# A state-space scan and a bilinear feed-forward on one core: longer down-weight rows, pair 2 turned later, seven small loads more

## The chip, the cores and the metric

The kernel runs on one core of one Trainium2 chip. Its time is the device time of one execution in microseconds (us); a version's time is the median over its runs. Five engines work side by side, each through its own instructions in order: TensorE (PE, with its weight loads shown as PEld), VectorE (DVE), ScalarE (ACT), GpSimd (POOL) and SyncE (SP), which here only issues DMAs. They meet at semaphores.

## The reference, cut to what matters

Inputs are `x` (4 batches, 8 heads, 768 steps, 32 wide), decays `a`, and `B`, `C` (16 states). The first part is a scan in chunks; per batch and head

```python
L = exp(cum[i] - cum[j]) * (i >= j)            # cum = cumsum(log a) in the chunk
y = (C @ B.T * L) @ x + (C @ state) * exp(cum)
state = decay_full * state + (B * decay_from_j).T @ x
```

The result, one row of 256 (8 heads of 32) for each of 3072 tokens, goes into a feed-forward part:

```python
a = y @ w_a          # 256 -> 1536
b = y @ w_b
out = (a * b) @ w_out   # 1536 -> 256
```

The order of the 1536 middle columns is free, as long as `w_a`, `w_b` and `w_out` agree on it.

## The kernel before

**Tiling.** A sequence is cut into 6 blocks of 128 steps, and two batches are taken together: 12 pairs `p` (`NP`), pair `p` being block `p // 2` of batches 2(p % 2) and the next. Per pair, in this order:

- `load(p)` (line 128): six DMAs on SP, two each for `bn`, `cn`, `xn` (64, 64 and 128 KB each). Three buffers of each.
- `scale(p)` (254): POOL multiplies `cn` and `bn` by the decay factors into `cm` and `bm` (in this order) and turns `xn` into f16.
- `transposes(p)` (259): four transposes on PE, of `bm` first, then `cm`. With `ct_first` DVE copies `ct` and then ACT writes `bt` in two operations; the `bt` operations wait for that `ct`.
- `scores(p)` (285): 32 small matmuls, which need `ct` and `bt`, into four banks `SC[0..3]`.
- `mask(product(p, m))` (318): DVE multiplies one bank by the causal mask; with `by_pool` ACT copies the bank out and POOL multiplies.
- `pv(p)` (362): PE forms the scan's output in the banks of `SC[2]` and `SC[3]`, so it starts after the masks of these have read them; then the sums for the state; then ACT writes `X2T` of the pair (line 383). `state(p)` follows on DVE and POOL.
- Six `unit(p, k2)` (462): 4 matmuls of 128x256 with `Wa` into a bank `aps`, 4 with `Wb` into `bps` (line 437), ACT copies `aps` to `asb` (451), DVE multiplies `bps` by `asb` into `hk` (458). `go` runs whole units. They need `X2T`.
- `out_mm` (468): 12 down products for each of the pair's two batches into a bank `ops`, `out_store` (480): ACT scales it into `osb`, SP stores it (488).

The banks `aps`, `bps`, `ops` are four of one pool (`psf`); a bank is used again when its last reader is done.

**Weights.** `Wa`, `Wb` are kept in halves of 768 columns, each loaded and cast by a POOL DMA (`load_w`), `Wo` in two halves of 6 x 256 (`load_wo`). Middle columns are dealt out so that a partition of `Wo` holds three neighbouring rows of `w_out` (3 KB in a row); the up products therefore pick every third column of `W` as their 128 weights:

```python
W[k // 6][:, f, k % 6 // 3 * 384 : (k % 6 // 3 + 1) * 384].rearrange("p (c kk) -> p kk c", kk=3)[:, k % 3]
```

**Order.** It is written out by hand (`manual_schedule`): each engine runs its instructions in the order in which the Python code records them, SP's DMAs too. Lines 590 to 627 hold the start-up of pairs 0 to 3, in which units of pairs 0 and 1 stand between the stages of pair 2; from line 629 a loop over `p` from 3 on repeats one pattern. SP's order in the start-up is: `x` of pair 2 (held until `Wb`'s second half has landed, line 579), `load(3)`, `load(4)`, the two stores of pair 0, `load(5)`, the two stores of pair 1, and so on.

Of the kernel before, what the change touches and what calls it, by code (L numbers as in the profile page):

```python
# [9 lines left out]
f32 = mybir.dt.float32  # L10
# [5 lines left out]
AFTER = mybir.DependencyInfo(mybir.DependencyClass.Sync, mybir.DependencyReason.DATA)  # L16
# [6 lines left out]
def kernel(  # L23
# [13 lines left out]
    nc = tc.nc  # L37
# [7 lines left out]
    NK = d_ff // 128  # L45
# [19 lines left out]
    const = ctx.enter_context(tc.tile_pool(name="const", bufs=1))  # L65
# [16 lines left out]
    Wo = big.tile([128, NK, d_model], f16, name="Wo")  # L82
# [37 lines left out]
    def load1(eng, p, which, bt, i0=0, n=64):  # L120
        blk, bp = divmod(p, NBP)
        src = (B, C, x)[which][2 * bp + bt, :, blk * Q + 2 * i0 : blk * Q + 2 * i0 + 2 * n, :]
        return eng.dma_start(  # L123
            pair_in[p][which][64 * bt + i0 : 64 * bt + i0 + n].rearrange("i h r n -> i h (r n)"),
            src.rearrange("h (i r) n -> i h (r n)", r=2),
        )

    def load(p, eng=None):
        tiles(p)
        return [load1(eng or nc.sync, p, w, bt) for w in range(3) for bt in range(2)]  # L130
# [7 lines left out]

    def load_wo(half):
        nc.gpsimd.dma_start(  # L140
            Wo[:, 6 * half : 6 * half + 6].rearrange("p (g kk) e -> p g (kk e)", kk=3),
            moe_w_out.rearrange("(g p kk) e -> p g (kk e)", p=128, kk=3)[:, 2 * half : 2 * half + 2],
        )

    nc.sync.dma_start(a_sb, a.rearrange("b h (k q) -> (b h) k q", q=Q))
# [36 lines left out]
    load1(nc.gpsimd, 1, 0, 1)  # L182
    load1(nc.gpsimd, 1, 1, 0)
    load_w(0)
    for bt in range(2):
        load1(nc.gpsimd, 1, 2, bt)

    def warmup(n, bank, cols=512):
        for _ in range(n):
# [69 lines left out]
    def transposes(p, ps=None, between=None, ct_first=False):  # L259
        s = st[p]  # L260
        TB, TC = (TT[:, 0:256], TT[:, 256:512]) if ps is None else [t_.bitcast(f16)[:, 0:256] for t_ in ps]
        for T_, src in ((TB, s["bm"]), (TC, s["cm"])):
            for r in range(2):
                nc.tensor.transpose(  # L264
                    T_[:, r * 128 : (r + 1) * 128], src[:, r].rearrange("p h n -> p (h n)"), ident
                )
            if between:
                between()
                between = None
        BT = mid.tile([128, 2, 2, 2, 64], f16, name="bt", tag="bt")  # L270
        CT = mid.tile([128, 2, Q], f16, name="ct", tag="ct")

        def ct(copy):
            copy(CT.rearrange("p t (i r) -> p r (t i)", r=2), TC.rearrange("p (r c) -> p r c", r=2))  # L274

        if ct_first:
            ct(nc.vector.tensor_copy)
        for e in range(2):
            o_ = BT[:, e].rearrange("p r t i -> p (r t i)")
            nc.scalar.activation(out=o_, in_=TB, func=AF.Copy, scale=par[:, e : e + 1])  # L280
        if not ct_first:
            ct(nc.scalar.copy if ps is None else nc.vector.tensor_copy)
        s["BT"], s["CT"] = BT, CT
# [20 lines left out]
    def product(p, m):  # L304

        return (
            st[p]["T1"][:, 2 * m : 2 * m + 2].rearrange("p e r q -> p e (r q)"),
            SC[m].rearrange("p (e c) -> p e c", e=2),
        )
# [8 lines left out]
    def mask(out_in, by_pool=False):  # L318
        o_, i_ = out_in
        c_ = causal.rearrange("p r q -> p (r q)").unsqueeze(1).broadcast_to((128, 2, 2 * Q))  # L320
        if by_pool:
            tmp = mid.tile([128, 2, 2 * Q], f32, name="tmp", tag="tmp")
            nc.scalar.copy(tmp, i_)
            nc.gpsimd.tensor_tensor(out=o_, in0=tmp, in1=c_, op=ALU.mult)
        else:
            nc.vector.tensor_tensor(out=o_, in0=i_, in1=c_, op=ALU.mult)  # L326
# [35 lines left out]
    def pv(p, then=None):  # L362
        blk, bp = divmod(p, NBP)
        s = st[p]
        PY = [SC1[:, bt, 0:256] for bt in range(2)]
        if blk > 0:
            for bt in range(2):
                for u in range(2):
                    nc.tensor.matmul(  # L369
                        PY[bt][:, u * Q : (u + 1) * Q],  # L370
                        s["Sbd"][:, bt, u * 128 : u * 128 + 128],
                        s["CT"][:, bt],
                        start=(u == 0),
                        stop=False,
                        skip_group_check=True,
                    )
        for u in range(2):
            pv_u(p, u, PY, blk == 0)
        if blk < NBLK - 1:
            ds_mm(p, 256)  # L380
        if then:
            then()
        nc.scalar.activation(  # L383
            out=X2T[:, p].rearrange("p u t q -> p t u q"),
            in_=SC1[:, :, 0:256].rearrange("p t (u q) -> p t u q", u=2),
            func=AF.Copy,
            scale=YS / XS,
        )
# [43 lines left out]
    def unit_mm(p, k2, W):  # L432
        ps = psf.tile([128, 512], f32, name="aps" if W is Wa else "bps", tag="ff")
        for kk in range(2):
            k = 2 * k2 + kk
            for f in range(2):
                nc.tensor.matmul(  # L437
                    ps[:, kk * 2 * Q : (kk + 1) * 2 * Q],
                    W[k // 6][:, f, k % 6 // 3 * 384 : (k % 6 // 3 + 1) * 384].rearrange("p (c kk) -> p kk c", kk=3)[
                        :, k % 3  # L440
                    ],
                    X2T[:, p, f].rearrange("p t q -> p (t q)"),
                    start=(f == 0),
                    stop=(f == 1),
                    skip_group_check=True,
                )
        return ps
# [14 lines left out]
    def unit(p, k2):  # L462
        a_ps = unit_mm(p, k2, Wa)
        b_ps = unit_mm(p, k2, Wb)
        asb = evac_a(a_ps)
        return lambda: times(p, k2, b_ps, asb)

    def out_mm(p, bt, o_ps, ks):
        hk = st[p]["hk"]
        for k in ks:  # L470
            nc.tensor.matmul(  # L471
                o_ps[:, 0:d_model],
                hk[:, k, bt * Q : (bt + 1) * Q],
                Wo[:, k, :],
                start=(k == 0),
                stop=(k == NK - 1),
                skip_group_check=True,
            )

    def out_store(p, bt, o_ps, on_dve=False, q=None):  # L480
        blk, bp = divmod(p, NBP)
        o_sb = ffh.tile([128, d_model], f32, name="osb", tag="osb")
        if on_dve:
            nc.vector.tensor_scalar(o_sb, o_ps[:, 0:d_model], 1.0 / (YS * YS), None, ALU.mult)
        else:
            nc.scalar.activation(out=o_sb, in_=o_ps[:, 0:d_model], func=AF.Copy, scale=1.0 / (YS * YS))  # L486
        r0 = (2 * bp + bt) * S + blk * Q
        (q or nc.sync).dma_start(out[r0 : r0 + Q, :], o_sb)
# [13 lines left out]
    def go(*items):  # L502
        for p, k2 in items:
            unit(p, k2)()
# [70 lines left out]
        op=ALU.mult,  # L575
    )
    load_wo(1)
    x2 = [load1(nc.sync, 2, 2, bt) for bt in range(2)]
    tc.add_manual_dep(x2[0].ins, w1[1].ins.name, AFTER, reason="weights ahead of pair 2's x")
    for m in range(3):  # L580
# [18 lines left out]
    state_spread(0)  # L599
    state_spread(1)  # L600
    load(3)
    go((0, 3), (0, 4))
    transposes(2, ct_first=True)
    go((1, 3), (0, 5))
    scores(2)
    mask(product(2, 3), by_pool=True)
    h = unit(1, 4)
    mask(product(2, 0))
    h()
    mask(product(2, 1))  # L610
    h = unit(1, 5)
    mask(product(2, 2))
    h()
    scale_x(2, nc.scalar)
    scale(3)
    o = [bank("ops"), bank("ops")]
    for bt in range(2):
        out_mm(0, bt, o[bt], range(6))
    pull(2)
    pv(2)  # L620
    transposes(3, ct_first=True)
    state(2)
    fb(2)
    load(4)
    for bt in range(2):
        out_mm(0, bt, o[bt], range(6, NK))
        out_store(0, bt, o[bt])

    for p in range(3, NP):
        scores(p)  # L630
        if p + 1 < NP:
            scale(p + 1)
        if p + 2 < NP:
            load(p + 2)
        h = unit(p - 1, 0)
        mask(product(p, 0))
        h()
        mask(product(p, 1))
        mask(product(p, 2))
        h = unit(p - 1, 1)  # L640
        h()
        mask(product(p, 3))
        go((p - 1, 2))
        out_half(p - 2, 0)
        go((p - 1, 3))
        pull(p)
        pv(p)
        state(p)
        if p + 1 < NP:
            transposes(p + 1)  # L650
        out_half(p - 2, 1)
        if p % 2 == 0 and p // 2 + 1 < NBLK:
            fb(p // 2 + 1)
        go((p - 1, 4), (p - 1, 5))
# [6 lines left out]
    o = [psf.tile([128, 512], f32, name="ops", tag="ff") for _ in range(2)]  # L661
# [35 lines left out]
```

## Time and profile before

| | |
|---|---|
| median of 10 runs | 132.12 us (131.57 to 132.68) |
| profiled execution | 132.39 us, its span 130.7 us |
| granted PE clock, mean | 0.996 |
| busy in the span | PE 124.0, PEld 105.5, DVE 88.2, ACT 74.1, POOL 57.5 us |
| DMA | 12.22 MB, mean 94 GB/s |
| up products, 576 of 128x256 | 277 and 273 ns each |
| down products, 288 of 128x256 | 273 ns each |
| `hk` on DVE, `asb` on ACT | 688 and 587 ns each |

Times are counted from the span's start. Matmuls are pipelined: the profile gives each 128x256 one some 273 ns, but in a dense stretch they start 109 ns apart, so their sum says more than the engine's time. In a timeline row the columns are start, duration, engine, line, operation, output<-inputs, form, count, and in brackets the engine's idle time before it and what ended it; a row can hold several instructions of a kind, and its duration is then from the first start to the last end. Rows with a q (`SPq`) are the issuing sequencer's. In a row of waits: who waited, for whom, us in total, times, longest.

### The profile page before, as it was taken

Reading aid. Unit: us, or ns where it says so; the run is one execution under the profiler, and the core shown is the slowest. Engines: PE = TensorE matmul, PEld = TensorE weight load, DVE = VectorE, ACT = ScalarE, POOL = GpSimd, SP = SyncE. Lnnn points to the kernel's source line nnn. Section 1 sums busy time; section 2 is a strip of 40 time slices with the busy share of each in tenths; the row PEclk is TensorE's granted clock in tenths of the full one; section 3 lists DMA queues with packets and bytes.
Section 4 is the critical chain, followed back from the end, with each engine's and each line's share of the span. In section 5 each row is a group of like instructions: output and inputs, shape, how many; then the busy total and the mean of one; then the engine's idle time right before and its main releaser. Section 6 shows DMA issues by size and latency. Waiting matters only on the chain.

```text
span 130.7 us, 4738 instructions
## 1 busy us (share of the span) xinstructions
PE 124.0 (95%) x1951; PEld 105.5 (81%) x1951; DVE 88.2 (67%) x166; ACT 74.1 (57%) x152; POOL 57.5 (44%) x81
## 2 busy tenths in 40 slices
PE   6999989898999999999999999999999999999980
PEld 2455788786988988998988988998998889899970
DVE  2587777596784975965966947948939929744440
ACT  1455645574648556576476576575476485464520
POOL 6979496947745608409319129029046000000000
PEclk9999999999999999999999999999999999999998
DMA  3999979966556562532533434514511110110102
GB/s 68 187 132 227 166 154 168 158 120 116 134 103 140 107 143 55 105 85 61 104 84 80 83 88 86 114 48 100 111 48 35 40 40 5 40 40 5 55 25 80
DMA packets 39333, 12.22 MB, mean 94 GB/s; under 512 B 34480, under 2 KB 39120, under 8 KB 39312
## 3 DMA queue, kind: packets, MB, share of 16 engines
q1 hardware_dynamic: 34832, 8.41, 29.3%
q0 software_dynamic: 1952, 3.02, 13.7%
q10 hardware_dynamic: 2528, 0.49, 2.1%
q8 instruction: 15, 0.25, 0.9%
q14 instruction: 6, 0.05, 0.1%
HBM read 11.13 MB, written 3.15 MB: 109 GB/s over the span
## 4 chain that ended last, share of the span: by engine, by line
PE 82%; DVE 7%; DMA 3%; issue 2%; ACT 2%; ACTq 1%
PE aps L437 23%; PE ops L471 22%; PE bps L437 20%; PE SC L293 4%; PE SC L335 3%; DMA cn<-in_C_dram 3%; PE SC L264 3%; DVE t L326 3%; DVE hk L458 2%; PE SC L369 2%; PE tc L190 2%; PE fps L216 1%; PE SC L352 1%; ACT bt L280 1%; ACTq L123 1%
## 5 line engine op out<-in xcount | busy, mean ns | idle before, releaser
L458 DVE TENSOR_TENSOR hk<-bps,asb 128x512 f16<-128x512 f32 x72 | 49.2, 688 | 25.1 <-ACT asb L451 22.3
L451 ACT COPY asb<-aps 128x512 f32<-128x512 f32 x71 | 41.6, 587 | 19.1 <-PE aps L437 16.9
L437 PE MATMUL aps<-X2T,Wa 128*128 128x256 f16 x288 | 43.8, 277 | 0.0
L437 PE MATMUL bps<-X2T,Wb 128*128 128x256 f16 x288 | 42.9, 273 | 0.0
L471 PE MATMUL ops<-Wo,hk 128*128 128x256 f16 x288 | 35.3, 273 | 0.0
L437 PEld LDWEIGHTS <-Wa 128*128 128x128 f16 x288 | 29.2, 105 | 3.3 <-issue 0.3
L437 PEld LDWEIGHTS <-Wb 128*128 128x128 f16 x288 | 29.6, 103 | 1.9
L326 DVE TENSOR_TENSOR t<-SC,causal 128x512 f16<-128x512 f32 x45 | 29.5, 682 | 2.2 <-PE SC L293 1.4
L471 PEld LDWEIGHTS <-hk 128*128 128x128 f16 x288 | 27.7, 98 | 3.2
L417 POOL TENSOR_TENSOR sbd<-U,maskbd 128x512 f16<-128x512 f32 x10 | 11.6, 1160 | 34.4 <-DVE U L410 25.2
L486 ACT ACTIVATE osb<-ops 128x256 f32<-128x256 f32 x23 | 8.8, 386 | 15.7 <-PE ops L471 15.7
L240 POOL TENSOR_SCALAR x<-xn 128x512 f16<-128x512 f32 x9 | 13.4, 1492 | 2.6 <-DMA xn<-in_x_dram 2.0
L383 ACT ACTIVATE X2T<-SC 128x512 f16<-128x512 f32 x11 | 6.6, 597 | 8.5 <-PE SC L352 7.6
L280 ACT ACTIVATE bt<-SC,ch 128x256 f16<-128x256 f16 x22 | 9.2, 472 | 1.9 <-DVE ct L274 1.5
L410 DVE SCALAR_TENSOR_TENSOR U<-SC,G,gU 128x64 f32<-128x64 f32 x16 | 3.8, 279 | 4.6 <-ACT X2T L383 4.6
L246 POOL TENSOR_TENSOR bm<-bn,fB 128x256 f16<-128x256 f32 x11 | 6.9, 624 | 0.0
L190 PE MATMUL SC<-warm 128*128 128x512 f16 (+1 forms) x15 | 5.6, 522 | 1.2 <-DVE warm L159 1.2
L246 POOL TENSOR_TENSOR cm<-cn,fC 128x256 f16<-128x256 f32 x10 | 6.2, 622 | 0.6 <-DMA cn<-in_C_dram 0.6
L293 PEld LDWEIGHTS <-bt 32*64 32x64 f16 x384 | 3.6, 108 | 3.0 <-issue 2.3
L293 PE MATMUL SC<-ct,bt 32*64 32x128 f16 x384 | 5.4, 227 | 0.6 <-ACT bt L280 0.5
L335 PEld LDWEIGHTS <-x 64*32 64x32 f16 x384 | 3.0, 91 | 3.2 <-ACT fC L536 0.8
L190 PEld LDWEIGHTS <-warm 128*128 128x128 f16 x21 | 2.4, 133 | 3.9 <-issue 2.6
(65 smaller groups left out, 80.4 us busy)
## 6 DMA issues: line engine op xcount, KB each, us to landing
out_dram<-osb SPq DMA_DIRECT2D x23, 128.0 KB, 1.7
xn<-in_x_dram SPq DMA_DIRECT2D x21, 128.0 KB, 3.2
bn<-in_B_dram SPq DMA_DIRECT2D x20, 64.0 KB, 2.6
cn<-in_C_dram SPq DMA_DIRECT2D x18, 64.0 KB, 2.6
Wa<-in_moe_w_a_dram POOLq DMA_DIRECT2D x2, 384.0 KB, 5.6
Wb<-in_moe_w_b_dram POOLq DMA_DIRECT2D x2, 384.0 KB, 7.1
Wo<-in_moe_w_out_dram POOLq DMA_DIRECT2D x2, 384.0 KB, 6.8
xn<-in_x_dram POOLq DMA_DIRECT2D x2, 128.0 KB, 6.8
```

Source lines behind the costliest of these rows:

```text
L190: nc.tensor.matmul(bank[:, 0:cols], warm[:, 0:128], warm[:, 0:cols], start=True, stop=True, skip_group_check=True)
L240: eng.tensor_scalar(xo, xi, XS, None, ALU.mult)
L246: eng.tensor_tensor(out=m_, in0=pair_in[p][which].rearrange("p h r n -> p r h n"), in1=f[:, blk, :, bp].unsqueeze(3).broadcast_to((128, 2, ...
L280: nc.scalar.activation(out=o_, in_=TB, func=AF.Copy, scale=par[:, e : e + 1])
L293: nc.tensor.matmul(SC[m][64 * bt : 64 * bt + 64, c0 : c0 + Q], BT[rows, e, r, bt], CT[rows, bt], start=True, stop=True, skip_group_check=True,
L326: nc.vector.tensor_tensor(out=o_, in0=i_, in1=c_, op=ALU.mult)
L417: nc.gpsimd.tensor_tensor(out=Sbd.rearrange("p t (m c) -> p t m c", m=4), in0=U32[:, p].unsqueeze(2).broadcast_to((128, 2, 4, 2 * D)), in1 ...
L437: nc.tensor.matmul(ps[:, kk * 2 * Q : (kk + 1) * 2 * Q], W[k // 6][:, f, k % 6 // 3 * 384 : (k % 6 // 3 + 1) * 384].rearrange("p (c kk) -> ...
L451: (nc.vector.tensor_copy if on_dve else nc.scalar.copy)(asb, a_ps)
L458: nc.vector.tensor_tensor(out=s["hk"][:, 2 * k2 : 2 * k2 + 2, :].rearrange("p k q -> p (k q)"), in0=b_ps, in1=asb, op=ALU.mult)
L471: nc.tensor.matmul(o_ps[:, 0:d_model], hk[:, k, bt * Q : (bt + 1) * Q], Wo[:, k, :], start=(k == 0), stop=(k == NK - 1), skip_group_check= ...
L486: nc.scalar.activation(out=o_sb, in_=o_ps[:, 0:d_model], func=AF.Copy, scale=1.0 / (YS * YS))
```

## The change

Four edits:

1. A partition of `Wo` holds six neighbouring rows of `w_out`: 6 KB in a row instead of 3 KB. The up products pick every sixth column of a half instead of every third of a quarter.
2. Seven loads of 14, 12, 10, 8, 6, 4 and 2 partitions by 64 bytes from `w_a` into a tile that nothing reads, on SP ahead of pair 2's `x`; the first waits for the second half of pair 1's `x`.
3. The transposes of pair 2 stand behind units (1,3) and (0,5); units (1,4) and (1,5) ahead of its scores; its masks follow each other with no `hk` between.
4. All 24 down products of pair 0 stand ahead of `pv(2)` (before: 12 ahead, 12 behind the transposes of pair 3), pair 0's two stores directly behind `pv(2)`, ahead of `load(4)`; unit (2,0) ahead of the loop and thus of `scores(3)`.

```diff
     def load_wo(half):
         nc.gpsimd.dma_start(
-            Wo[:, 6 * half : 6 * half + 6].rearrange("p (g kk) e -> p g (kk e)", kk=3),
-            moe_w_out.rearrange("(g p kk) e -> p g (kk e)", p=128, kk=3)[:, 2 * half : 2 * half + 2],
+            Wo[:, 6 * half : 6 * half + 6].rearrange("p kk e -> p (kk e)"),
+            moe_w_out.rearrange("(g p kk) e -> p g (kk e)", p=128, kk=6)[:, half],
         )
...
-    for bt in range(2):
-        load1(nc.gpsimd, 1, 2, bt)
+    x1 = [load1(nc.gpsimd, 1, 2, bt) for bt in range(2)]
...
-                    W[k // 6][:, f, k % 6 // 3 * 384 : (k % 6 // 3 + 1) * 384].rearrange("p (c kk) -> p kk c", kk=3)[
-                        :, k % 3
-                    ],
+                    W[k // 6][:, f].rearrange("p (c kk) -> p kk c", kk=6)[:, k % 6],
...
     load_wo(1)
+    pz = const.tile([16, 7, 16], f32, name="pz")
+    for i, k in enumerate((14, 12, 10, 8, 6, 4, 2)):
+        d = nc.sync.dma_start(pz[0:k, i], moe_w_a[0:k, 0:16])
+        if i == 0:
+            tc.add_manual_dep(d.ins, x1[1].ins.name, AFTER, reason="probe")
     x2 = [load1(nc.sync, 2, 2, bt) for bt in range(2)]
...
     load(3)
-    go((0, 3), (0, 4))
+    go((0, 3), (0, 4), (1, 3), (0, 5))
     transposes(2, ct_first=True)
-    go((1, 3), (0, 5))
+    go((1, 4), (1, 5))
     scores(2)
     mask(product(2, 3), by_pool=True)
-    h = unit(1, 4)
-    mask(product(2, 0))
-    h()
-    mask(product(2, 1))
-    h = unit(1, 5)
-    mask(product(2, 2))
-    h()
+    for m in range(3):
+        mask(product(2, m))
     scale_x(2, nc.scalar)
     scale(3)
     o = [bank("ops"), bank("ops")]
-    for bt in range(2):
-        out_mm(0, bt, o[bt], range(6))
+    for ks in (range(6), range(6, NK)):
+        for bt in range(2):
+            out_mm(0, bt, o[bt], ks)
     pull(2)
     pv(2)
+    for bt in range(2):
+        out_store(0, bt, o[bt])
     transposes(3, ct_first=True)
     state(2)
     fb(2)
     load(4)
-    for bt in range(2):
-        out_mm(0, bt, o[bt], range(6, NK))
-        out_store(0, bt, o[bt])
+    go((2, 0))
 
     for p in range(3, NP):
...
-        h = unit(p - 1, 0)
+        h = unit(p - 1, 0) if p > 3 else None
         mask(product(p, 0))
-        h()
+        if h:
+            h()
```

## The prediction

> **What bounds the kernel now.** I read the page first (busy times and the 40 slices), then the windows, the waits, and last the timeline from 14 to 47 us with the order in which each engine's instructions stand. "PE's place" below is the moment at which PE could start its next matmul: matmuls of 128x256 start 0.109 us apart and the profile lets each last 0.273, so half a unit (4 matmuls) moves PE's place by 0.437 us and 12 down products move it by 1.31.
>
> ```profile
> PE 124.0 (95%) x1951; PEld 105.5 (81%) x1951; DVE 88.2 (67%) x166; ACT 74.1 (57%) x152; POOL 57.5 (44%) x81
> PE   6999989898999999999999999999999999999980
> ```
>
> TensorE sets the time. From 33 us on no slice shows a hole, so whatever delays PE there is kept to the end, and whatever is saved earlier is kept too.
>
> ```profile
> 0.00:18.27 18.27, 16.18 (x261) 9.44 (x261) 11.88 (x30) 8.36 (x18) 14.54 (x28) 1.00 0.94 161
> 18.27:32.53 14.26, 13.25 (x195) 11.49 (x191) 10.37 (x23) 8.73 (x19) 10.30 (x16) 1.00 0.80 135
> 32.53:37.71 5.18, 5.18 (x76) 4.76 (x76) 4.18 (x7) 2.82 (x7) 3.98 (x5) 1.00 0.52 125
> 37.71:130.70 92.99, 89.37 (x1426) 79.84 (x1423) 61.77 (x108) 54.21 (x110) 28.67 (x34) 0.99 0.31 72
> ```
>
> Columns: window, length, busy time of PE, PEld, DVE, ACT, POOL, clock, DMA share, GB/s. The second window is the one that the change rearranges; the third is already dense, and the fourth's shortfall is the few per cent of missing records and the end.
>
> ```profile
> 24.35 0.44 DVE L274 COPY ct<-SC 128x256 f16<-128x256 f16 x1
> 24.82 0.84 ACT L280 ACTIVATE bt<-SC,ch 128x256 f16<-128x256 f16 x2 [1.37 <-DVE ct L274]
> 28.57 1.28 DVE L326 TENSOR_TENSOR t<-SC,causal 128x512 f16<-128x512 f32 x2
> 28.76 1.27 SPq L123 DMA_DIRECT2D bn<-in_B_dram  x2
> 29.90 0.38 PE L369 MATMUL SC<-ct,sbd 128*128 128x128 f16 x4 [0.38 <-DVE t L326]
> 30.87 0.60 ACT L383 ACTIVATE X2T<-SC 128x512 f16<-128x512 f32 x1 [1.95 <-PE SC L352]
> 32.37 0.66 ACT L486 ACTIVATE osb<-ops 128x256 f32<-128x256 f32 x2
> 32.97 2.42 SPq L488 DMA_DIRECT2D out_dram<-osb  x2
> ```
>
> PE's holes in that window: 0.64 us before `scores(2)` (its place is 25.07, `bt` ends at 25.66, scores start at 25.71), 0.54 before `pv(2)` (29.36 to 29.90, the last mask), 0.26 before `scores(3)` (32.27 to 32.53, `bt` again). 1.44 us is all that a better order could find. The other thing to see is SP: `load(4)` is issued from 28.76, ahead of pair 0's two stores at 32.97.
>
> ```profile
> SPq L488 <- ACT osb L486: 46.9, 18, 5.7
> cn<-in_C_dram SPq DMA_DIRECT2D x18, 64.0 KB, 2.6
> ```
>
> SP takes its DMAs in order and stands at the stores for 46.9 us in all. What stands behind a store waits with it.
>
> **The new order, step by step.** All up to unit (0,4) is as before (PE's place 23.10). Rows used: in a chain DVE's 128x512 operations start 0.60 apart and last 0.68; `asb` copies last 0.59, 0.47 apart; an engine starts 0.03 to 0.05 after its releaser ends.
>
> PE now does (1,3) at 23.10 and (0,5) at 23.97 without the four transposes between; the banks are free in time (the closest by 0.04 us). Transposes of pair 2 at 24.85, (1,4) at 25.07, (1,5) at 25.94, place 26.82. DVE: `hk` of (1,3) at 24.35, of (0,5) at 25.23 (behind its `asb`, 25.20), then `ct` 25.83 to 26.27. ACT: the two `bt` 26.30 to 27.14. Scores(2) at 27.19: a hole of 0.37 where 0.64 was. `bt` stands before the copies of (1,4) and (1,5) on ACT, so these run at 27.03 and 27.50, end 27.62 and 28.08. The first down bank is the one of (1,4)'s `aps`: down products from 27.67, all 24 of pair 0, place 30.29 (24 x 0.109). Both halves of `Wo` have landed by 27.65 in the trace, the second is asked for at 28.98. DVE meanwhile: `hk` of (1,4) 27.64, of (1,5) 28.24, three masks 28.84, 29.44, 30.04 to 30.72. `pv(2)` at 30.77, where it was 29.90: 0.87 later with 12 products (1.31) more behind it, 0.44 ahead.
>
> Then it is given back. `X2T` stood 0.97 after `pv(2)` and lasts 0.60: 31.74 to 32.34. Unit (2,0), now ahead of `scores(3)`, needs it: 32.39 against a place of 31.82, 0.57 idle. Its 8 matmuls end at a place of 33.27. On ACT the two `osb` (0.26 apart, 32.23 and 32.50, ends 32.62 and 32.89) now stand before `bt` of pair 3: 32.77 to 33.61, scores(3) at 33.66, 0.39 idle. From there: (2,1) 34.02, (2,2) 34.89, 12 down products 35.77, (2,3) 37.08, `pv(3)` at 37.95 (it was 37.71), transposes of pair 4 possible at 37.95 + 0.82 = 38.77; they were at 38.54. DVE's last mask of pair 3 ends at 37.78, in time. So the order by itself costs **+0.23 us**.
>
> **Its loads cost more.** `load(4)` is recorded after `out_store(0)` now: six DMAs behind two stores. First `osb` ends 32.62: store 32.65, second store about 33.07 (0.34 each plus 0.09, as the later stores at 46.84 and 50.09), `bn` from 33.50 instead of 28.76. Issues stand 0.67 apart, so `cn`'s second half is issued at 35.50 and lands 2.6 later, 38.10. POOL takes `cm` first, in order: 38.20, then `bm` 38.78 to 39.40 (0.58 apart, 0.62 long); before, `bm` of pair 4 was done at 35.27, 3.3 us early. The transposes wait for `bm`: 39.45 against 38.54. PE stands 0.68 us at them, behind them `out_half(1)` and units (2,4), (2,5). Place of all later work: **+0.91 us**. Bounds: landings of 2.4 to 3.1 us in single rows give 0.7 to 1.4. I take the median's. The next pairs are not caught: pair 5's `cn` lands near 42.3, its `bm` is done by 44.5, its transposes come at 49.
>
> The row of 2.6 us decides that term. The Trainium skill, "DMA: Bandwidth & Descriptors", section "Anatomy of one DMA", fits 2.0 us plus bytes over 436 GB/s for GpSimd's DMAs; for 64 KB that would be an estimated 2.15 us and the sum +0.46.
>
> **Other edits.** *Probes*: SP is idle from 4.9 to 18.75 us, where pair 2's `x` waits for `Wb`'s second half (18.73). The first probe waits for pair 1's `x` (14.35 in the trace); seven issues at 0.34 (a store) to 0.63 (a load) end at 16.7 to 18.8. Hidden by that wait: 0. Without that cover pair 2's `x` would come at most 4.4 us later, against 28.5 where ACT wants it (it lands 24.5 and 27.0). *`Wo` in 6 KB rows*: 512 packets of 1536 bytes (135 ns) become 256 of twice that (between 135 and the 230 ns of 4096 bytes, 192): (512 x 135 - 256 x 192) / 16 = 1.3 us less for each DMA engine in a stretch that is 80% full. What lands earlier then (pair 2's `x`, pair 3's load) is wanted later anyway: 0, and no loss shorter than 0.6 us, the time by which pair 3's `bm` precedes its transposes.
>
> *Weights at a step of 6*: every up product now loads its 128 columns 12 bytes apart instead of 6. The weight loads of `hk` (step 1) last 98 ns, those of `Wa`, `Wb` (step 3) 103, both hidden under 109 ns of matmul. A line through these gives 110.5 at step 6: if that became the pace, 576 x 1.3 ns = 0.75 us. If the longest row of an exposed load did (152 ns): 576 x 43 ns = 24.7 us. A quicker load gains nothing under 109. I take 0: four packed transposes 56 ns apart show that a load's duration is not its pace.
>
> One rule speaks against this edit: the Trainium skill, "SBUF — State Buffer", section "Specifications (TRN2)", asks for at least two hits in each 16-byte line for full bandwidth. At step 3 a line holds 2.7 of the f16 weights wanted, at step 6 1.3, so by it the weight loads slow down; it gives no price.
>
> **Sum.** 132.39 us is the profiled execution's own time (span 130.7, 1.7 around it); with 0.91 it is 133.30. It lies 0.27 above the median of the ten runs, so against 132.12 the forecast is **133.0 us**.
>
> **Rivals.** (1) *Pair 4's load is covered*: if `cn` lands by 37.4 (1.9 us after its issue, or stores released 0.7 earlier) `bm` meets PE at 38.77 and +0.23 remains: 132.35, no change. For it: SP has nothing else queued then. Against it: no `cn` row lands under 2.4. Chance 0.14. (2) *Weight loads set the pace*: everywhere, from the first unit. 0.91 + 0.75 gives 133.8, up to 157. For it 103 over 98; against it the matmul spacing, the same for `Wa` and `hk`. Chance 0.20. (3) *Order gains*: the masks end early enough to close the 0.48 hole before `pv(2)` and the 0.39 before scores(3), and the load is covered: 0.23 - 0.87 = -0.64, 131.5. Against it: the stores move with `pv(2)`, so 0.48 earlier still leaves +0.43 at the transposes. Chance 0.08. (4) *The change doesn't do what it says*: the probes wait longer than the weights do and hold pair 2's `x`; this is inside the 0.20 and 0.58, since they'd only add. The forecast itself: 0.58.
>
> **The numbers.** About 0.3% (0.4 us) can be told from no change: faster is under 131.7, slower over 132.5. Slower: 0.58 + 0.20 = 0.78; same 0.14; faster 0.08. The range runs from below (1), 132.1, to (2) at its low price on top of late landings (1.4 + 0.75), 134.3; what it leaves out is (3) and dear weights, some 0.2.
>
> **What would show it.** Right: POOL's `cm` of pair 4 idle until a DMA, `bn` issued after the first two stores, PE's only hole past 34 us at the transposes of pair 4, near 39. Right about the order: idle PE before (2,0) and scores(3). Wrong: up products more than 109 ns apart; a dense PE at 38 to 40; pair 2's `x` issued well after 18.8 us; holes in the first 18 us.

## The result, and the profile after

| | before | after |
|---|---|---|
| median | 131.91 us (50 runs) | 133.0 us (15 runs, 132.44 to 135.77) |
| ratio | | 1.0092, 95% interval 1.0066 to 1.0118 |
| profiled execution, its span | 132.39, 130.7 us | 132.93, 131.2 us |

The changed kernel is 0.9% slower. It takes the 133.0 us of the forecast, but the forecast added 0.91 to 132.12, the median of 10 runs, and against the 131.91 of 50 runs the change costs 1.09. Medians here are over all runs, while ratios leave out disturbed ones, mostly with PE at half clock for a while; of the profiled executions below `e2`, `e8`, `e9` and `e10` are disturbed (in `e8` the half clock lies ahead of (1,0), in `e2` and `e9` behind T4, in `e10` between (1,0) and T3, so its value for that way is in brackets).

The busy times and PE's slices of the page after:

```profile
PE 122.6 (93%) x1951; PEld 108.8 (83%) x1951; DVE 88.1 (67%) x166; ACT 74.3 (57%) x152; POOL 57.6 (44%) x81
PE   6998899988969999999999999999999999999980
```

PE has the same 1951 matmuls, and its weight loads are 3.3 us longer. The twelfth slice, 36.1 to 39.4 us, reads 6 where it read 9. The windows (length, busy PE, PEld, DVE, ACT, POOL, clock, DMA share, GB/s) put the loss in the same place: in the last, PE's busy time is 4.79 us short of the length, and it was 3.62 before, 1.17 more; in the second it is 1.23 short where it was 1.01.

```profile
18.27:32.53 14.26, 13.03 (x212) 11.67 (x217) 9.72 (x21) 8.68 (x19) 8.93 (x13) 1.00 0.68 122
32.53:37.71 5.18, 5.04 (x120) 4.58 (x103) 4.88 (x8) 2.45 (x6) 1.45 (x3) 1.00 0.52 103
37.71:131.20 93.49, 88.70 (x1372) 82.12 (x1372) 61.08 (x107) 53.99 (x109) 31.14 (x36) 0.99 0.32 74
```

The timeline from 17 to 47 us shows it whole:

```profile
29.40 0.38 PE L368 MATMUL SC<-ct,sbd 128*128 128x128 f16 x4 [0.34 <-DVE t L325]
30.52 0.29 PE L263 MATMUL SC<-ident,bm 128*128 128x128 f16 x2 [0.23 <-POOL bm L245]
31.27 0.86 SPq L485 DMA_DIRECT2D out_dram<-osb  x2
32.23 1.37 SPq L123 DMA_DIRECT2D bn<-in_B_dram  x2
32.34 0.43 PE L292 MATMUL SC<-ct,bt 32*64 32x128 f16 x32 [0.29 <-ACT bt L279]
33.70 1.92 SPq L123 DMA_DIRECT2D cn<-in_C_dram  x2
36.67 0.39 PE L368 MATMUL SC<-ct,sbd 128*128 128x128 f16 x4
37.61 0.62 POOL L245 TENSOR_TENSOR cm<-cn,fC 128x256 f16<-128x256 f32 x1 [3.73 <-DMA cn<-in_C_dram]
38.19 0.62 POOL L245 TENSOR_TENSOR bm<-bn,fB 128x256 f16<-128x256 f32 x1
38.86 0.29 PE L263 MATMUL SC<-ident,bm 128*128 128x128 f16 x2 [1.30 <-POOL bm L245]
```

Read it from the last row upwards. PE stands 1.30 us at the transposes of pair 4 for `bm`; POOL made `bm` late because its `cm`, which comes first, had idled 3.73 us for the DMA; that load was issued from 33.70 because it stands in SP's order behind pair 0's stores, which could leave only when `osb` was there, at 31.27. This is the chain of the forecast, link by link.

### The profile page after: what moved, and what is told of

Its sections match the earlier page's. It is cut to its first block, busy times and chain, and to the rows that moved or that the text cites. A ratio compares the mean times of both kernels' runs of the same rounds, so it can differ in the third digit from the quotient of the medians.

```text
span 131.2 us, 4745 instructions
## 1 busy us (share of the span) xinstructions
PE 122.6 (93%) x1951; PEld 108.8 (83%) x1951; DVE 88.1 (67%) x166; ACT 74.3 (57%) x152; POOL 57.6 (44%) x81
## 3 DMA queue, kind: packets, MB, share of 16 engines
q0 software_dynamic: 1696, 3.02, 13.8%
## 4 chain that ended last, share of the span: by engine, by line
PE 78%; DMA 6%; DVE 5%; POOL 4%; issue 2%; ACT 2%; SPq 0%; POOLq 0%; ACTq 0%
PE aps L436 24%; PE bps L436 21%; PE ops L468 21%; DMA Wa<-in_moe_w_a_dram 5%; DVE t L325 3%; PE SC L292 3%; PE SC L334 3%; PE SC L263 2%; DMA cn<-in_C_dram 2%; PE SC L368 2%; PE SC L351 1%; DVE hk L455 1%; ACT bt L279 1%; POOL causal L179 1%; PE fps L215 1%
## 5 line engine op out<-in xcount | busy, mean ns | idle before, releaser
L436 PEld LDWEIGHTS <-Wa 128*128 128x128 f16 x288 | 31.7, 126 | 1.9 <-DMA Wa<-in_moe_w_a_dram 0.6
L436 PEld LDWEIGHTS <-Wb 128*128 128x128 f16 x288 | 32.5, 125 | 0.5 <-DMA Wb<-in_moe_w_b_dram 0.5
L416 POOL TENSOR_TENSOR sbd<-U,maskbd 128x512 f16<-128x512 f32 x10 | 11.7, 1166 | 29.6 <-DVE U L409 24.1
```

The costliest lines, as they stand in the source:

```text
L416: nc.gpsimd.tensor_tensor(out=Sbd.rearrange("p t (m c) -> p t m c", m=4), in0=U32[:, p].unsqueeze(2).broadcast_to((128, 2, 4, 2 * D)), in1 ...
L436: nc.tensor.matmul(ps[:, kk * 2 * Q : (kk + 1) * 2 * Q], W[k // 6][:, f].rearrange("p (c kk) -> p kk c", kk=6)[:, k % 6], X2T[:, p, f].rea ...
```

## The experiments

Milestones: "T3", "T4" are the first transposes of pairs 3 and 4 on PE; "(1,0)" is PE's first matmul of unit (1,0), which marks the end of the start-up.

| run | ratio to before (95%) | (1,0) | T3 | T4 | (1,0) to T4 | period of a pair |
|---|---|---|---|---|---|---|
| before | | 18.27 | 30.72 | 38.54 | 20.27 | 9.39 |
| after | 1.0092 (1.0066, 1.0118) | 16.84 | 30.52 | 38.86 | 22.02 | 9.41 |
| `e1`: after, load early | 0.9982 (0.9946, 1.0018) | 16.86 | 30.25 | 37.54 | 20.68 | 9.41 |
| `e2`: before, load late | 1.0116 (1.0076, 1.0156) | 16.93 | 30.28 | 40.64 | 23.71 | 9.39 |
| `e3`: rows alone | 1.0007 (0.9965, 1.005) | 16.75 | 30.13 | 37.96 | 21.21 | 9.41 |
| `e4`: seven loads alone | 0.9991 (0.995, 1.0032) | 17.95 | 30.39 | 38.21 | 20.26 | 9.39 |
| `e5`: order alone, load late | 1.0136 (1.0085, 1.0187) | 17.86 | 31.20 | 40.46 | 22.60 | 9.39 |
| `e6`: order alone, load early | 0.9997 (0.9961, 1.0032) | 17.14 | 30.47 | 37.67 | 20.53 | 9.39 |
| `e7`: before, once more | (one run) | 18.93 | 31.37 | 39.19 | 20.26 | 9.39 |
| `e8`: order carried on | 0.9941 (0.9901, 0.998) | 19.08 | 32.00 | 38.81 | 19.73 | 9.39 |
| `e9`: `e8`, a mask on POOL | 1.0053 (1.0004, 1.0103) | 17.22 | 30.13 | 38.96 | 21.74 | 9.39 |
| `e10`: that mask earlier | 0.9898 (0.9864, 0.9932) | 17.88 | 32.36 | 38.71 | (20.83) | 9.39 |

**The late load, undone.**

```diff
     pv(2)
+    load(4)
     for bt in range(2):
         out_store(0, bt, o[bt])
...
-    load(4)
     go((2, 0))
```

> The changed kernel with load(4) issued ahead of pair 0's two stores again; everything else of the change stays. Theory (late load): PE's 1.3 us hole before the transposes of pair 4 goes, what stays is the order's own 0.2 us and some 0.2 us of weights: 132.1 to 132.4 where the kernel before has 131.9, ratio 1.001 to 1.004. Rival (weight loads or the order set the loss): no better than the change, ratio 1.007 to 1.010, and the time from the transposes of pair 4 to the end stays what it was.

Measured: 131.52 us (6 runs). With one line moved the whole loss is gone; the order's own 0.2 us, which the theory left in it, does not show either (ratio 0.9982). In its timeline from 28 to 44 us the stores come after the load, POOL starts `cm` of pair 4 four microseconds earlier, and PE does not stand at pair 4's transposes:

```profile
32.08 1.05 SPq L485 DMA_DIRECT2D out_dram<-osb  x2
33.65 0.62 POOL L245 TENSOR_TENSOR cm<-cn,fC 128x256 f16<-128x256 f32 x1
37.54 0.29 PE L263 MATMUL SC<-ident,bm 128*128 128x128 f16 x2
```

From (1,0) to T4 it takes 20.68 us against 22.02 in the changed kernel: the late load costs 1.34 there.

**The late load alone**, in the kernel before.

```diff
-    load(4)
     for bt in range(2):
         out_mm(0, bt, o[bt], range(6, NK))
         out_store(0, bt, o[bt])
+    load(4)
```

> The kernel before with nothing but load(4) moved behind pair 0's two stores. Theory (late load): the second store is issued near 33.6 us, bn of pair 4 near 34.2 instead of 28.8, POOL's bm of pair 4 ends near 39.8 and PE stands some 1.2 us at the transposes of pair 4: ratio 1.007 to 1.010. Rival (late load is covered): no hole there, ratio within 0.002 of 1.

Measured: 133.61 us (6 runs), ratio 1.0116. One moved line makes the kernel before as slow as the changed one. Here the stores come at the end of the down products as before, so the load is later still, and PE stands 2.48 us, twice what was expected (timeline from 33 to 45 us). This execution took 136.17 us; by the ratio the moved line costs 1.5 us, and how long PE stands in the other runs is not on record.

```profile
33.28 2.60 SPq L123 DMA_DIRECT2D bn<-in_B_dram  x2
39.39 0.62 POOL L246 TENSOR_TENSOR cm<-cn,fC 128x256 f16<-128x256 f32 x1 [5.90 <-DMA cn<-in_C_dram]
40.64 0.28 PE L264 MATMUL SC<-ident,bm 128*128 128x128 f16 x2 [2.48 <-POOL bm L246]
```

**The rows alone**: the kernel before with `Wo` in 6 KB rows and the up products' weights at a step of 6.

```diff
-            Wo[:, 6 * half : 6 * half + 6].rearrange("p (g kk) e -> p g (kk e)", kk=3),
+            Wo[:, 6 * half : 6 * half + 6].rearrange("p kk e -> p (kk e)"),
...
-                    ...rearrange("p (c kk) -> p kk c", kk=3)[:, k % 3],
+                    W[k // 6][:, f].rearrange("p (c kk) -> p kk c", kk=6)[:, k % 6],
```

> The kernel before with nothing but the 6 KB rows of the down weights, so up products load their weights at a step of 6. Theory (weights stay hidden behind the matmuls, only the first load after a stage is exposed): the dense period of 9.39 us becomes 9.41, 0.2 us in all, ratio 1.000 to 1.003. Rival (weight loads set the pace): matmuls over 109 ns apart, ratio 1.006 or more.

Measured: 132.20 us, ratio 1.0007. The groups of weight loads (count | busy us, mean ns of one | idle) of the kernel before and then of this run:

```profile
L437 PEld LDWEIGHTS <-Wb 128*128 128x128 f16 x288 | 29.6, 103 | 1.9
```

```profile
L437 PEld LDWEIGHTS <-Wb 128*128 128x128 f16 x288 | 32.5, 125 | 0.3 <-DMA Wb<-in_moe_w_b_dram 0.2
L469 PEld LDWEIGHTS <-hk 128*128 128x128 f16 x288 | 27.7, 98 | 3.0
```

A load at step 6 takes 125 ns, and that is longer than the 109 ns from one matmul to the next. The matmuls nevertheless stay 109 ns apart (the median, in both), and a pair takes 9.41 us instead of 9.39: 0.2 us over the kernel, which the ratio does not resolve.

**The seven loads alone.**

```diff
+    pz = const.tile([16, 7, 16], f32, name="pz")
+    for i, k in enumerate((14, 12, 10, 8, 6, 4, 2)):
+        d = nc.sync.dma_start(pz[0:k, i], moe_w_a[0:k, 0:16])
...
```

> The kernel before with nothing but the seven small loads. Theory: their issues end some 1.5 us before Wb's second half lands, nothing waits: ratio 0.998 to 1.002. Rival (they hold pair 2's x or slow the weights' transfers): x of pair 2 issued later than 18.8 us, or the first 18 us longer, ratio 1.004 or more.

Measured: 131.83 us, ratio 0.9991. SP's own timeline of this run:

```profile
15.74 2.46 SPq L579 DMA_DIRECT2D pz<-in_moe_w_a_dram  x7
19.43 1.35 SPq L123 DMA_DIRECT2D xn<-in_x_dram  x2
20.87 1.27 SPq L123 DMA_DIRECT2D bn<-in_B_dram  x2
```

The seven issues end at 18.20; what follows waits for `Wb` until 19.43 and would wait without them.

**The order alone, load early.** The kernel before with the change's parts 3 and 4, except that `load(4)` is recorded ahead of the stores; no long rows, no seven loads.

> The kernel before with the new order alone (transposes of pair 2 two units later, all 24 down products of pair 0 ahead of pv(2), unit (2,0) ahead of scores(3)), load(4) still ahead of the stores, rows of 3 KB, no small loads. Prediction's step (the order costs 0.23 us): ratio 1.001 to 1.003. Theory since the first runs (in executions whose first units start near 17 us the old order waits for pair 3's bm, the new one hides that): 0.3 to 0.5 us gained, ratio 0.995 to 0.998, and transposes of pair 4 at 20.5 us or less after unit (1,0), where the old order needs 21.2 in such an execution.

Measured: 131.84 us (12 runs), ratio 0.9997. PE needs 20.53 us from (1,0) to T4 where the kernel before needs 20.27. So the order by itself costs 0.26 us by this path and gains nothing that the medians show: the theory's 0.3 to 0.5 us did not come. What the order does is told below.

**The kernel before, once more**, unchanged, to see whether its start-up differs between executions.

> The kernel before, unchanged, for a second profile. Theory (the start differs from execution to execution): unit (1,0) starts anywhere from 16.7 to 18.3 us; if near 17, PE waits for POOL's bm of pair 3 at its transposes and the time from unit (1,0) to pair 4's transposes is some 21.2 us instead of 20.3. Rival (the start is a trait of the kernel): unit (1,0) at 18.3 again, 20.3 from there.

Measured: one run, 133.05 us, (1,0) at 18.93, later than the theory's 16.7 to 18.3, and 20.26 us from there to T4, the profile of before again but for a later start. A quick start of the old order is to be seen in `e2` and `e3` only, which share it up to T3.

**The order alone, load late.** As `e6`, with one line moved:

```diff
-    load(4)
     for bt in range(2):
         out_store(0, bt, o[bt])
...
+    load(4)
     go((2, 0))
```

> The kernel before with the change's new order alone (Wo in 3 KB rows, no seven loads), with load(4) behind pair 0's two stores as the change has it; against the earlier run with load(4) ahead of the stores it differs in that one line. Theory (the late load is the whole loss, 0.9 to 1.5 us, whatever the rows and the seven loads are): POOL's cm of pair 4 waits for a DMA, PE stands 0.7 to 1.4 us at the transposes of pair 4, from unit (1,0) to these 21.3 to 22.0 us, median 0.9 to 1.4 us over the kernel before, ratio 1.007 to 1.011. Rival (the seven loads hold up SP's or the DMA engines' later work and are part of why the load lands so late): the six issues go quicker, cn's second half lands over 0.5 us earlier after the first store than in the changed kernel, the wait is under 0.7 and the ratio under 1.005.

Measured: 134.16 us, ratio 1.0136. Timeline from 38 to 46 us:

```profile
39.20 0.62 POOL L246 TENSOR_TENSOR cm<-cn,fC 128x256 f16<-128x256 f32 x1 [5.08 <-DMA cn<-in_C_dram]
40.46 0.29 PE L264 MATMUL SC<-ident,bm 128*128 128x128 f16 x2 [1.99 <-POOL bm L246]
```

The rival falls: without the seven loads the second half of `cn` is issued 3.94 us after the first store (36.18 against 32.24), with them 3.72. The theory's mechanism holds and its size was too small: 1.99 us of wait, and 22.60 - 20.53 = 2.07 us on the path. Half of what this run has over the changed kernel's 1.34 is a later landing, 3.02 us from that issue to `cm` instead of 2.62.

**The order carried on.** If the holes of the order (0.34 us before `pv(2)`, 0.29 before `scores(3)`) can be closed, it should win. Three masks of pair 2 go ahead of the `hk` of (1,4) and (1,5) on DVE, 6 of the 24 down products go behind `pv(2)`, units (2,0) and (2,1) ahead of `scores(3)`, `load(4)` ahead of the stores (cut, against `e6`).

```diff
     transposes(2, ct_first=True)
-    go((1, 4), (1, 5))
+    h4, h5 = unit(1, 4), unit(1, 5)
     scores(2)
     mask(product(2, 3), by_pool=True)
     for m in range(3):
         mask(product(2, m))
+    h4()
+    h5()
...
     pv(2)
+    out_mm(0, 1, o[1], range(6, NK))
...
-    go((2, 0))
+    go((2, 0), (2, 1))
```

> The order carried further from the kernel before: pair 2's masks ahead of hk of (1,4) and (1,5) on DVE, 18 down products of pair 0 ahead of pv(2) and 6 behind it (they fill the wait for X2T), units (2,0) and (2,1) ahead of scores(3), load(4) ahead of the stores, 3 KB rows, no small loads. Theory (after load(4) the masks and X2T set the rest): PE's holes before pv(2), unit (2,0) and scores(3) shrink to under 0.3 us each, one of 0.4 stays before pv(3), ratio 0.993 to 0.997. Rival (pair 3's load sets the start-up whatever the order): no better than the order alone.

Measured: 131.40 us (12 runs), ratio 0.9941: faster than both kernels. What is left of waiting on PE past `scores(2)` is 0.29 us before `pv(3)`, for the fourth of pair 3's masks, which DVE now does in one chain (timeline from 34 to 40 us):

```profile
35.47 2.47 DVE L326 TENSOR_TENSOR t<-SC,causal 128x512 f16<-128x512 f32 x4
37.99 0.38 PE L369 MATMUL SC<-ct,sbd 128*128 128x128 f16 x4 [0.29 <-DVE t L326]
```

**One of these masks on POOL**, recorded behind `scale(4)`, which is where the loop has its masks.

```diff
+        if p == 3:
+            mask(product(p, 3), by_pool=True)
+            for m in range(3):
+                mask(product(p, m))
```

> As the one before, and the last mask of pair 3 goes through ACT and POOL instead of DVE. Theory: DVE is done with pair 3's masks 0.6 us earlier, the hole before pv(3) goes, ratio 0.990 to 0.995. Rival: POOL or ACT is late with it, or the pair 4 scaling behind it on POOL makes pair 4's transposes wait: no better than without it.

Measured: 133.72 us (12 runs), ratio 1.0053. A failure: POOL takes its instructions in order, and the mask stood behind pair 4's `x`, which waited 0.71 us for its own DMA and lasted 1.49 (timeline from 33 to 41 us):

```profile
35.90 1.49 POOL L240 TENSOR_SCALAR x<-xn 128x512 f16<-128x512 f32 x1 [0.71 <-DMA xn<-in_x_dram]
37.47 1.15 POOL L324 TENSOR_TENSOR t<-tmp,causal 128x512 f16<-128x512 f32 x1
38.67 0.29 PE L335 MATMUL SC<-t,x 64*32 64x128 f16 x12 [2.36 <-POOL t L324]
```

**The same mask ahead of `scale(4)`.**

```diff
         if p == 3:
             mask(product(p, 3), by_pool=True)
         if p + 1 < NP:
             scale(p + 1)
...
         if p == 3:
-            mask(product(p, 3), by_pool=True)
             for m in range(3):
```

> The order that was faster than the kernel before, with the last mask of pair 3 on POOL as in the slower run, but recorded ahead of pair 4's scaling on POOL instead of behind it. Theory (the slower run lost its time only because POOL's mask stood behind the scaling of pair 4 and PE's 2.4 us wait was followed by half clock): the mask on POOL is done about 2.5 us earlier, PE does not stand at pv(3), no half clock follows, and the time is that of the faster order or 0.1 to 0.3 us better: ratio 0.990 to 0.997. Rival (POOL becomes the bound there: cm and bm of pair 4 now come after the mask, 1.2 us later): pair 4's transposes wait, PE stands 0.5 to 1 us there instead, ratio 0.998 to 1.003.

Measured: 130.41 us (9 runs, 129.57 to 132.57), ratio 0.9898 (0.9864 to 0.9932): the fastest of all. The timeline from 34 to 40 us:

```profile
35.71 1.16 POOL L324 TENSOR_TENSOR t<-tmp,causal 128x512 f16<-128x512 f32 x1 [0.34 <-ACT tmp L323]
35.82 1.88 DVE L326 TENSOR_TENSOR t<-SC,causal 128x512 f16<-128x512 f32 x3
37.88 0.39 PE L369 MATMUL SC<-ct,sbd 128*128 128x128 f16 x4
38.71 0.29 PE L264 MATMUL SC<-ident,bm 128*128 128x128 f16 x2
```

POOL's mask is done at 36.87, DVE's three at 37.70, and PE stands at neither `pv(3)` nor T4. From T3 to T4, a way that the start-up leaves alone (7.82 us in the kernel before, `e4` and `e7`, with (1,0) at 18.27, 17.95 and 18.93), PE needs 7.20 us in `e6`, 6.81 in `e8` and 6.35 in `e10`, for the same work in all three. The expected rival, POOL as the bound, did not come: `bm` of pair 4 is done at 38.03, before its transposes.

## Why the prediction was right, point by point

**The cause** was right, and is shown from both sides: taken out of the changed kernel the late load gives back the whole loss (`e1`), put alone into the kernel before it makes a loss of the same size (`e2`), and with the new order alone it does so again (`e5` against `e6`, one line apart).

**Its size** was half of what it is: 0.68 us of wait forecast, 1.30 measured in the changed kernel (1.99 and 2.48 in the other two). The step that failed is SP's train of issues. The forecast put the second half of `cn` 2.85 us after the first store (32.65 to 35.50); it was issued 3.72 us after it (31.27 to 34.99). Up to `cn`'s first issue only 0.24 us had gathered (2.43 after the first store against 2.19), but that issue lasted 1.24 us instead of 0.63. Why single issues take so long is not settled; SP's timelines of the kernel before have them as well (1.75 us for one store at 33.63), so the median that was used was too kind for a train on the path. The landing of that issue is not in the trace; from the issue to `cm` it took 2.62 us (34.99 to 37.61), where the forecast had 2.70 (35.50 to 38.20). The Trainium skill, "DMA: Bandwidth & Descriptors", section "Anatomy of one DMA", would have given an estimated 2.15 by its fit for GpSimd's DMAs; these are SP's, and the runs have 2.6 and 3.0 up to the reader.

**The order** was forecast step by step from (1,0) on, and all of it but the load held within 0.22 us:

| after (1,0), us | forecast | changed kernel |
|---|---|---|
| `pv(2)` | 12.50 | 12.56 |
| unit (2,0) | 14.12 | 14.18 |
| `scores(3)` | 15.39 | 15.50 |
| `pv(3)` | 19.68 | 19.83 |
| PE ready for T4 (38.86 less the 1.30 of its row) | 20.50 | 20.72 |
| `bm` of pair 4 done | 21.13 | 21.97 |

Its +0.23 is the 0.26 by which `e6` needs longer from (1,0) to T4 than the kernel before, yet `e6` is not slower. What the forecast did not see: (1,0) itself comes anywhere from 16.75 to 19.08 us. The three latest are those with PE at half clock in the start-up: `e7` and `e8` from 11.7 or 11.8 us for 3.4 us, and the profile of the kernel before until 13.6. Its granted clock reads 1.00 there, but its matmuls of 128x256 start 0.213 us apart, and the first twelve take 2.16 us where the changed kernel's take 1.51 (timelines of the two up to 17 us):

```profile
12.21 2.16 PE L437 MATMUL aps<-X2T,Wa 128*128 128x256 f16 x12
```

```profile
11.42 1.51 PE L436 MATMUL aps<-X2T,Wa 128*128 128x256 f16 x12 [0.24 <-DMA Wa<-in_moe_w_a_dram]
```

At full clock (1,0) still comes from 16.75 to 17.95. The forecast took the 18.27 of that one execution. Where the start is quick, the old order reaches T3 before `bm` of pair 3 is there, and PE stands (0.84 us in `e2`); so in `e3`, from 28 to 34 us:

```profile
30.13 0.29 PE L264 MATMUL SC<-ident,bm 128*128 128x128 f16 x2 [0.82 <-POOL bm L246]
```

From (1,0) to T4 that run needs 21.21 us, 0.68 more than `e6`. So the new order loses 0.26 in slow starts and wins up to 0.68 in quick ones; the ratio of `e6`, 0.9997 with 0.35% to either side, can't show which prevails. The slack of 0.6 us that the forecast gave pair 3's `bm` was likewise that of a slow start: in the changed kernel PE stood 0.23 there.

With these the two profiled spans close: from before to after (1,0) is 1.43 earlier (0.65 of it in the twelve matmuls above), (1,0) to T4 is 1.75 longer, and from T4 to the end it is 0.18 longer (92.34 against 92.16, the 0.02 per pair). That makes +0.50, and 130.7 becomes 131.2. By the medians the change costs 1.09: a late load of 1.3 to 1.5 (1.34 on the path, 133.0 - 131.52 = 1.48 by medians), less what the order may win in quick starts, which is argued and within the intervals. The forecast's +0.91 is near it because its two errors, a load too cheap and, by the medians, an order too dear, have opposite signs: the mechanism was right, but that the number came so close is partly luck.

**The seven loads and the long rows** were put at 0: `e4` and `e3` agree with that within their 0.5%. The packets of 3072 bytes were dearer than estimated, a median of 248 ns instead of 192 in the traces of the changed kernel and `e3`, so the rows save each DMA engine (512 x 135 - 256 x 248) / 16 = 0.35 us and not 1.3; no time was built on that. **The weights**: the line through 98 and 103 ns gave 110.5, measured 125. So the condition of rival (2) was met and passed, and its price did not come: the duration of a load is not its pace. The Trainium skill's rule of two hits per line ("SBUF — State Buffer", section "Specifications (TRN2)") fits the loads' duration, 98, 103 and 125 ns at 8, 2.7 and 1.3 hits, and what the longer loads cost is no more than 0.02 us per pair here. Its page "TensorE: Matmul & The Clock Gate", section "Architectural detail: the array is 16× 32×32, not 1× 128×128", says that a matmul can begin before its weight load completes, which would fit; that is not shown here by itself.

**The signs to look for**: `cm` idle until a DMA, `bn` issued behind the stores, and a hole at pair 4's transposes at 38.86 all came; idle PE before `scores(3)` and before unit (2,0) came too. The rows count it from the modelled end of the matmul before, the forecast from PE's place, which is 0.16 us earlier: by that measure it is 0.45 before `scores(3)` (0.29 in the row, forecast 0.39), and before unit (2,0) 0.57 in `e5` and `e6` (0.40 in their rows, forecast 0.57), in the changed kernel 0.28 behind the 0.23 lost at T3. Rival (3), that the order gains, came true only in kernels that take it further.

## What to carry to other kernels

A queue that issues in order has a price list: when a store moves ahead of a load, the load starts when the store's data are ready, and everything up to its landing, its scaling and its first reader must fit into the slack that is left; add up the train of issues with its slow ones in it, not with the median. A gain of PE time ahead of a chain of other engines was here only a loan until that chain (the masks, then `bt` behind `osb`, then `bm`) was shortened too, and moving a step to another engine paid only at the right place in that engine's order: the same POOL mask held PE for 2.36 us behind pair 4's scaling and, ahead of it, took 0.46 us off the path. Forecast from more than one execution where the start-up varies, since a slack read in a slow one may not be there in a quick one.

## What the runs showed of the hardware that was not expected

A hole on PE may cost more than its length. After the holes of 2.48 us (`e2`) and 2.36 us (`e9`) PE ran at half clock for one stretch of 3.4 us, and the next pair took 11.06 and 11.03 us instead of 9.39. The windows of `e9` around it (the column after POOL's is the granted clock):

```profile
35.60:38.94 3.34, 0.98 (x54) 0.65 (x52) 1.16 (x2) 0.46 (x1) 2.64 (x2) 1.00 0.49 91
38.94:42.36 3.42, 3.42 (x39) 2.54 (x20) 0.48 (x2) 1.86 (x5) 1.86 (x3) 0.50 0.53 127
```

The runs speak for a link: 7 of the 12 of `e9` have a mean clock of 0.987 or less, and 5 of the 29 of the kernel before that were taken beside them; by the medians of all runs `e9` is 1.84 us slower than it. After the holes of 1.30 us (changed kernel) and 1.99 us (`e5`) the clock stayed full: there PE was busy for 2.17 and 1.47 us of the 3.4 ahead of the restart, while ahead of the fall of the clock it was busy for 0.98 here and for 0.93 in `e2`. But such a stretch also came without a long hole: in `e7`, the kernel before, behind 3.4 us in which PE was busy for 2.57 and never idle for more than 0.6 at a time, and in `e10` behind 3.4 us with 2.15 busy. So neither the hole nor the busy time by itself tells when the clock falls, and what does is open. The Trainium skill, "TensorE: Matmul & The Clock Gate", section "HAM oscillation — how this bites in real kernels", names idle gaps of over 3.4 us; here the clock fell after gaps of 2.4 us. Two of the changed kernel's 15 runs took 135.4 and 135.8 us at a lower mean clock, which would fit such a stretch; no profile shows one of them.
